# Holding batch 2's loads behind an exponential, and regrouping batch 1's last query turns and scores

## The chip, the core and the metric

The kernel runs on one core of one Trainium2 chip. A core has five engines with a queue each, taken in order: TensorE (PE, matmuls and transposes; PEld is its weight load), VectorE (DVE), ScalarE (ACT), GpSimd (POOL) and SyncE (SP). Here SP and POOL mainly issue DMAs, which 16 DMA engines carry out. The metric is the device time of one launch in microseconds (us): a median of runs, and beside it one profiled execution from which all rows of the trace come.

## The reference

Inputs are `q`, `k`, `v` of 4 batches, 8 heads, 768 tokens, 64 channels, and two weights. Each batch goes through a sparse attention: a token sees the tokens less than 16 away and 24 block summaries (the maximum of 32 keys, the mean of 32 values). A two-layer network with a sigmoid GELU follows.

```python
k_sum = k.reshape(B, H, nb, block, D).max(axis=3)
v_sum = v.reshape(B, H, nb, block, D).mean(axis=3)
mask_l = np.abs(pos[:, None] - pos[None, :]) < window
...
a = np.exp(scores_all)          # local scores (masked) and block scores, less their maximum
a = a / (np.sum(a, axis=-1, keepdims=True) + 1e-09)
out = np.matmul(a, v_all)
...
h = x @ w_in                    # x: tokens x 512, w_in 512 x 2048
g = h * (1.0 / (1.0 + np.exp(-1.702 * h)))
return (g @ w_out)              # w_out 2048 x 512
```

## The kernel before

The four batches are worked one after another, and the attention of a batch is spread among the matmuls of the network for the batch before it. PE has no holes that way. The order of every engine is the order of the program: each wrapped engine (`pe`, `dve`, `act`, `pool`, `sp`) keeps it, and the program writes it out with slots.

Heads are taken in four pairs p = 0 to 3, tokens in two halves of 384. For one batch and one pair:

- `load_batch(b)` issues the loads of a batch on POOL: four for the keys (`load_turned` into two tiles `kb`), twelve for the values (`load_v` into `vw`, one for each of six steps of 128 tokens and each half step), four for the queries (`load_turned` into two tiles `qb`). Before batch 3's loads a one-element copy on POOL into `gate2` reads what a DMA writes, so that POOL waits for it and its loads start no sooner.
- `tq(p, s, eng)` turns the queries of a pair of batch 1 on PE (six transposes into PSUM `ps_t`) and copies them to `qT` on DVE. For batches 2 and 3 `xk` and `xq` turn keys and queries by transposing DMAs on SP, from `kb` into `kx` and from `qb` into `qT`.
- `scores(b, half, p)` makes 12 matmuls into PSUM `ps_s` (two buffers in `psb`, shared by other work) and the exponential on ACT into a tile `a_sb[half, p]`. `mask(half, p)` multiplies that tile in place on DVE. `values(b, half, g)` multiplies two pairs with `vw` on PE and divides on DVE.
- `value_rows(s)` completes `vw` once it is loaded: `halo_dmas` on SP copies edge rows (`vw<-vw`), `vsum` sums blocks of 32 values on PE into `ps_vs` (48 matmuls, six steps of 128 tokens with 8 each), `block_sums` adds them on DVE, and `sum_dmas` spreads them with SP (`vw<-vs`).

The change lies in the output layer of the second half of batch 0, `ff_out(1, ms, part)`: twelve slots of four matmuls into `po`, three row tiles of four parts. After the fourth part of a row tile ACT copies it to `osb` and SP stores it. After each slot `beside(1, i)` does what the table `plan1` names for that slot: `t2` is `tq(2)`, `s02` is `scores` of half 0 and pair 2, `m02` its mask, `v00` the values of half 0 and group 0, `x..` turns of results. After slot 2 the program calls `load_batch(2)`, and after slots 9 and 11 `xk` for the two key tiles of batch 2.

Then the loop over batches begins with b = 1: `ff_open` and `ff_one` are its first layer (`ph`), `value_rows(0)` comes at its second step, `xq` for both query tiles at its third, and `rest_k` (maxima and edges of the keys) at its third to sixth. At its end come batch 2's first scores.

Of the kernel before, what the change touches and what calls it, by code (L numbers as in the profile page):

```python
# [35 lines left out]
def kernel(  # L36
# [30 lines left out]
    pool = _Ordered(tc, nc.gpsimd)  # L67
# [55 lines left out]
    def load_turned(x, b, t2, name, gs_=(0, 1)):  # L123

        for g in gs_:
            t2[g] = castp2.tile([128, 2, NJ, 2, D], BF16, name=name, tag=name)
            for hh in range(2):
                h0 = hh * NP + 2 * g
                pool.dma_start(out=t2[g][:, :, :, hh].rearrange("p i a d -> p (i a) d"),
                               in_=x[b, h0:h0 + 2].rearrange("h (a p) d -> p (h a) d", p=128))  # L130

    def load_v(b):
        w5 = vw[b % 2].rearrange("p (j e) h c -> p j e h c", e=2)
        src = v[b].rearrange("h (j e p) d -> e j p h d", e=2, p=64)
        for j in range(NJ):
            for e in range(2):
                pool.dma_start(out=w5[e * 64:e * 64 + 64, j, e, :, 0:D], in_=src[e, j])
# [106 lines left out]
            eng.memset(v6[g * 32:g * 32 + nb, :, g, D:D + 1], float(block))  # L244

    def load_batch(b):
        if b == 3:
            pool.tensor_copy(out=gate2, in_=qTs[0][:, 0, 0:1])
        load_turned(k, b, kb2, "kb")
        if b == 3:  # L250
            pool.tensor_copy(out=gate2, in_=qTs[0][:, NP - 1, 0:1])
        if b == 1:
            load_turned(q, b, qb2, "qb", (0,))
        load_v(b)
        if b < 3:
            load_turned(q, b, qb2, "qb", (1,) if b == 1 else (0, 1))
# [310 lines left out]
    def xk(g, s):  # L567
        k4 = kxs[s].rearrange("p i (j e) c -> p (i j) e c", e=2)
        src = kb2[g].rearrange("p i a h d -> p (i a h d)")
        for e in range(2):  # L570
            sp.dma_start(out=k4[:, 2 * g * NJ:2 * (g + 1) * NJ, e, e * 64:e * 64 + 64],
                         in_=src[e * 64:e * 64 + 64], transpose=True)
# [13 lines left out]
    a_sb, x_sb, x2 = {}, {}, {}  # L586
# [282 lines left out]
    def ff_out(u, ms, part):  # L869
        if part == 0:  # L870
            po_now[ms] = pmm.tile([128, d_model], F32, name="po", tag="mm")
        po = po_now[ms]
        for nt in range(4 * part, 4 * part + 4):
            pe.matmul(out=po, lhsT=gT[u % 2][:, nt, ms * 128:(ms + 1) * 128],
                      rhs=w_out_sb[:, nt, :], start=(nt == 0), stop=(nt == NT - 1))
        if part == 3:
            osb = outp.tile([128, d_model], F32, name="osb", tag="osb")
            act.activation(out=osb, in_=po, func=ACT.Copy)
            r0 = u * HALF + ms * 128
            sp.dma_start(out=out[r0:r0 + 128, :], in_=osb)  # L880

    gate = consts.tile([128, 2], F32, name="gate")
    gate2 = consts.tile([128, 1], BF16, name="gate2")
# [130 lines left out]
    for e in range(2):  # L1014
        r = slice(64 * e, 64 * e + 64)
        dve.tensor_copy(out=w50[r, JH - e:NJ, e, :, 0:D],
                        in_=v0n[r, :, JH - e:NJ, 0:D].rearrange("p h j d -> p j h d"))
# [3 lines left out]
    for p in range(NP):  # L1021
# [3 lines left out]
    dve.memset(vw[1][:, :, :, D:VC], 1.0)  # L1025
    clear_values(dve, 1)
    load_batch(1)


    plan0 = {1: ["q0", "q1", "q2"], 2: ["s0", "s1", "q3", "m0", "m1"], 4: ["s2", "s3", "m2", "m3"], 6: ["v0", "v1"], 8: ["x0"], 9: ["x1"]}  # L1030

    plan1 = {-1: ["s00", "s01"], 1: ["t2", "m00", "m01"], 2: ["t3", "s02"], 3: ["s03", "m02"], 4: ["m03", "s10"],
             5: ["s11", "m10"], 6: ["v00", "m11", "s12", "s13"], 7: ["v01", "g"], 8: ["m12", "m13"],
             9: ["x00", "x01", "v10"], 10: ["v11"], 11: ["x10"]}

# [20 lines left out]
    def beside(b, slot):  # L1056
        for what in (plan1 if b == 1 else plan).get(slot, ()):
            half, i = int(what[1:2] or 0), int(what[-1:] if len(what) > 1 else 0)
            if what[0] == "t":
                tq(i, 1, dve)  # L1060
            elif what[0] == "m":
                mask(half, i)
            elif what[0] == "g":
                gelu_soon()
            elif what[0] == "R":
                value_rows(1)
            elif what[0] == "s":
                scores(b, half, i)
            elif what[0] == "v":
                values(b, half, i)  # L1070
            elif what[0] == "d":
                dx(half, i)
            else:
                tx(half, i)
# [38 lines left out]
    for i, (ms, part) in enumerate((ms, part) for ms in range(JH) for part in range(4)):  # L1113
        ff_out(1, ms, part)
        beside(1, i)
        if i == 2:
            load_batch(2)
        if i in (9, 11):
            xk(i // 2 - 4, 0)
# [3 lines left out]
    for b in range(1, B - 1):  # L1123
# [32 lines left out]
        i = 0  # L1156
        for t, what in seq:
            product(b, t, what)
            if i == 0:
                g_sums(NT // 2 - 1, dve, (2, 3))  # L1160
            if nxt:
                beside(b + 1, i)
            i += 1
            if nxt and b + 2 < B:
                if i == 1:
                    load_batch(b + 2)
                if i in (16, 18):
                    xk(i // 2 - 8, b % 2)
# [4 lines left out]
    b, n = B - 1, NT // 2  # L1173
# [82 lines left out]
```

## Time and profile before

| what | value |
|---|---|
| median of 3 runs | 205.96 us (205.91 to 206.78) |
| profiled execution, its own time | 205.39 us |
| span of the profile | 203.4 us |
| PE / DVE / ACT / POOL busy | 97% / 69% / 62% / 44% |
| mean granted PE clock | 0.998 |
| output stage with the change (slots 0 to 11) | about 58.2 to 74.5 us of the span |

The span runs from the first to the last instruction of the program; the execution's own time holds 2.0 us more around it. Rows of a timeline give the start and the length in us, the engine, the operation, the tiles (out<-in) and how many were merged, and in brackets the idle time of the engine ahead of them and what ended it. Nearly all instructions carry line 28, the helper that records them, so they are told apart by their tiles. SPq is SP's queue of DMA issues: the length there is that of the issue, not of the transfer.

### The profile page before, as it was taken

The page shows a single profiled execution, that of the slowest core. Times are in us where ns is not written, and L with a number is a line of the kernel's source. Part 1 is how long each engine was busy: PE and PEld are TensorE (multiplying, and loading weights), DVE is VectorE, ACT ScalarE, POOL GpSimd, SP SyncE. Part 2 cuts the span into 40 slices and gives each one's busy share as a digit, 9 for nine tenths or more (in the row PEclk, how much of TensorE's full clock was granted, in tenths as well). Part 3 has the DMA queues.
Part 4 walks back from the last instruction along what each step waited for, and adds up shares of the span by engine and source line. Part 5 has one row for each costly group of instructions (what it writes and reads, how often), then busy time and mean ns, then how long its engine had stood idle before and what let it go on. Part 6 is the DMA issues. An engine that isn't in the chain of part 4 may idle for free.

```text
span 203.4 us, 5851 instructions
## 1 busy us (share of the span) xinstructions
PE 196.7 (97%) x2358; PEld 136.6 (67%) x2358; DVE 141.2 (69%) x391; ACT 125.4 (62%) x240; POOL 89.9 (44%) x141
## 2 busy tenths in 40 slices
PE   6889999999999999999999999999999999999993
PEld 5548655556754566655888876666888865578882
DVE  6586894694856884898767789896769567758221
ACT  4584976638786717777871446778670559984220
POOL 7964489447899584000986034000000009980000
PEclk9999999999999999999999999999999999999999
DMA  5999999999999999999999979999022930000223
GB/s 171 169 165 204 207 207 215 189 156 243 116 122 170 176 170 178 127 165 155 114 181 156 173 140 139 110 247 179 0 104 62 185 119 3 0 0 0 106 105 103
DMA packets 95994, 28.13 MB, mean 138 GB/s; under 512 B 83664, under 2 KB 93152, under 8 KB 95968
## 3 DMA queue, kind: packets, MB, share of 16 engines
q0 software_dynamic: 69648, 13.24, 84.8%
q1 hardware_dynamic: 26176, 14.39, 34.8%
q8 instruction: 18, 0.29, 0.6%
q10 hardware_dynamic: 144, 0.13, 0.2%
q14 instruction: 8, 0.07, 0.1%
HBM read 27.26 MB, written 6.29 MB: 165 GB/s over the span
## 4 chain that ended last, share of the span: by engine, by line
PE 91%; DMA 3%; DVE 3%; issue 1%; ACT 0%; POOLq 0%; DVEq 0%
PE ph L28 32%; PE poA L28 16%; PE po L28 11%; PE poB L28 7%; PE phA L28 4%; PE ps_av L28 4%; PE poC L28 4%; PE ps_s L28 3%; DMA qe<-in_q_dram 3%; DVE ks L28 2%; PE ps_t L28 1%; PE ps_x L28 1%; PE phC L28 1%; PE phB L28 1%; PE phE L28 1%; DVE qT L28 1%
## 5 line engine op out<-in xcount | busy, mean ns | idle before, releaser
L28 PE MATMUL ph<-xT,w_in_sb 128*128 128x384 f16 x400 | 67.8, 326 | 0.1
L28 PEld LDWEIGHTS <-w_in_sb 128*128 128x128 f16 x442 | 42.7, 98 | 27.2 <-issue 0.2
L28 ACT ACTIVATE gT<-ph 128x384 f16<-128x384 f32 x100 | 47.9, 491 | 18.4 <-PE ph L28 17.6
L28 PEld LDWEIGHTS <-gT 128*128 128x128 f16 x312 | 28.8, 98 | 11.3 <-issue 0.2
L28 ACT ACTIVATE a_sb<-ps_s 128x768 bf16<-128x768 f32 (+1 forms) x32 | 25.0, 826 | 12.0 <-PE ps_s L28 12.0
L28 PEld LDWEIGHTS <-gs 128*128 128x128 f16 x288 | 27.7, 98 | 3.4
L28 POOL DMA_DIRECT2D vw<-in_v_dram x36 | 24.6, 699 | 11.9 <-DMA kb<-in_k_dram 5.4
L28 POOL TENSOR_TENSOR gs<-gT 128x384 f16<-128x384 f16 x8 | 7.3, 911 | 43.3 <-ACT gT L28 43.2
L28 PE MATMUL po<-w_out_sb,gT 128*128 128x512 f16 x96 | 23.6, 380 | 0.0
L28 PE MATMUL poA<-ws,gs 128*128 128x256 f16 x144 | 18.7, 273 | 0.0
L28 DVE TENSOR_TENSOR a_sb<-a_sb,mk 128x768 bf16<-128x768 bf16 x28 | 14.9, 554 | 5.5 <-ACT a_sb L28 5.0
L28 DVE TENSOR_TENSOR x<-ps_av,rc 128x384 f16<-128x384 f32 x32 | 17.8, 557 | 1.1
L28 DVE TENSOR_TENSOR gs<-gT 128x384 f16<-128x384 f16 (+1 forms) x34 | 13.3, 390 | 7.2 <-ACT gT L28 6.9
L28 POOL DMA_DIRECT2D qb<-in_q_dram x16 | 15.1, 961 | 2.5 <-DMA w_in_sb<-in_moe_w_in_dram 1.2
L28 PEld LDWEIGHTS <-kx 64*128 64x128 bf16 (+1 forms) x378 | 9.9, 95 | 6.8 <-issue 3.6
L28 POOL DMA_DIRECT2D kb<-in_k_dram x14 | 13.6, 986 | 0.3 <-issue 0.3
L28 DVE TENSOR_REDUCE ks<-kx 128x24 bf16<-128x768 bf16 x12 | 11.4, 948 | 3.4 <-ACT kx L28 3.2
L28 ACT ACT_TABLE_LOAD x10 | 12.8, 1283 | 1.0 <-PEq L1240 0.8
L28 ACT ACTIVATE osb<-poA 128x256 f32<-128x256 f32 x9 | 3.5, 384 | 16.1 <-PE poA L28 16.1
L28 ACT ACTIVATE s<-poA 128x256 f32<-128x256 f32 x11 | 4.2, 385 | 11.2 <-PE poA L28 11.2
L28 PEld LDWEIGHTS <-a_sb 128*64 128x64 bf16 (+2 forms) x400 | 7.9, 108 | 2.8 <-issue 1.3
L28 PE MATMUL poA<-ws,gT 128*128 128x256 f16 x72 | 9.3, 273 | 0.0
(117 smaller groups left out, 288.2 us busy)
## 6 DMA issues: line engine op xcount, KB each, us to landing
out_dram<-osb SPq DMA_DIRECT2D x22, 256.0 KB, 3.9
kb<-in_k_dram POOLq DMA_DIRECT2D x14, 192.0 KB, 6.6
qb<-in_q_dram POOLq DMA_DIRECT2D x12, 192.0 KB, 10.5
vw<-in_v_dram POOLq DMA_DIRECT2D x36, 64.0 KB, 5.5
w_out_sb<-in_moe_w_out_dram POOLq DMA_DIRECT2D x4, 512.0 KB, 12.8
w_in_sb<-in_moe_w_in_dram POOLq DMA_DIRECT2D x3, 512.0 KB, 12.4
vw<-vs SPq DMA_DIRECT2D x6, 198.0 KB, 6.6
gT<-in_k_dram SPq DMA_DIRECT2D x2, 384.0 KB, 3.4
```

The costliest lines, as they stand in the source:

```text
L28: r = f(*a, **kw)
```

## The change

Three edits. In `load_batch`, batch 2's loads get a gate of their own: a one-element POOL copy that reads the exponentials of half 0, pair 2. `load_batch(2)` is called a slot later, after slot 3 instead of slot 2, since those exponentials now come in slot 3. In `plan1` the query turns of pairs 2 and 3 stand together in slot 2 (before: slots 1 and 2), the scores of pairs 2 and 3 together in slot 3 (before: slots 2 and 3), and the masks of both in slot 4 (before: slots 3 and 4), beside the first scores of the other half.

```diff
     def load_batch(b):
+        if b == 2:
+            pool.tensor_copy(out=gate2, in_=a_sb[0, 2][:, 0, 0, 0:1])
         if b == 3:
             pool.tensor_copy(out=gate2, in_=qTs[0][:, 0, 0:1])
         load_turned(k, b, kb2, "kb")
...
-    plan1 = {-1: ["s00", "s01"], 1: ["t2", "m00", "m01"], 2: ["t3", "s02"], 3: ["s03", "m02"], 4: ["m03", "s10"],
+    plan1 = {-1: ["s00", "s01"], 1: ["m00", "m01"], 2: ["t2", "t3"], 3: ["s02", "s03"], 4: ["m02", "m03", "s10"],
              5: ["s11", "m10"], 6: ["v00", "m11", "s12", "s13"], 7: ["v01", "g"], 8: ["m12", "m13"],
              9: ["x00", "x01", "v10"], 10: ["v11"], 11: ["x10"]}
...
         ff_out(1, ms, part)
         beside(1, i)
-        if i == 2:
+        if i == 3:
             load_batch(2)
         if i in (9, 11):
             xk(i // 2 - 4, 0)
```

## The prediction

> **What bounds the kernel now.** I read the page first, then the chain of waits through batch 1's output stage, then POOL, ACT and SP in order of time, then the DMA answers for single issues.
>
> ```profile
> span 203.4 us, 5851 instructions
> PE 196.7 (97%) x2358; PEld 136.6 (67%) x2358; DVE 141.2 (69%) x391; ACT 125.4 (62%) x240; POOL 89.9 (44%) x141
> PEclk9999999999999999999999999999999999999999
> DMA  5999999999999999999999979999022930000223
> ```
>
> TensorE sets the time: it is busy for 97% of the span, at full clock. So an edit can gain only by taking work off PE, and loses when PE has to wait. The DMA engines are busy in nearly every slice of the first 60%, which is where the change works. The chain of waits there (start, length, what):
>
> ```profile
> 58.22 1.83 PE po L28 x8
> 60.06 0.34 PE ps_t L28 x6
> 60.39 0.86 PE po L28 x4
> ...
> 61.59 0.28 PE ps_s L28 x12
> 61.87 0.97 PE po L28 x4
> 62.84 0.28 PE ps_s L28 x12
> ...
> 70.85 0.67 PE ps_x L28 x12
> ...
> 80.33 0.53 PE ps_vs L28 x48
> 80.86 15.71 PE ph L28 x96
> 96.56 0.46 PE ps_s L28 x24
> ```
>
> It is PE from end to end. Two places in it take data from batch 2's loads: `ps_vs` at 80.33 sums the freshly loaded values (vsum), and `ps_s` at 96.56 needs the turned queries. PE takes its work in order, so at either place a late load stops everything behind it. POOL, which issues the loads, in order of time:
>
> ```profile
> 58.49 0.45 POOL L28 COPY kx<-ks 128x288 bf16<-128x288 bf16 x1
> 58.86 4.04 POOL L28 DMA_DIRECT2D kb<-in_k_dram  x4
> ...
> 72.92 1.37 POOL L28 DMA_DIRECT2D vw<-in_v_dram  x2 [0.92 <-DMA vw<-in_v_dram]
> 74.25 4.08 POOL L28 DMA_DIRECT2D qb<-in_q_dram  x4
> 95.86 0.19 POOL L28 COPY gate<-qT 128x1 bf16<-128x1 bf16 x1 [17.53 <-DMA qT<-qb]
> 96.38 4.04 POOL L28 DMA_DIRECT2D kb<-in_k_dram  x4 [0.32 <-issue]
> ...
> 106.45 3.40 POOL L28 DMA_DIRECT2D vw<-in_v_dram  x5 [0.48 <-DMA vw<-in_v_dram]
> ```
>
> Batch 2's loads start at 58.86, as soon as POOL has built batch 1's keys, and the last of twelve value loads is issued at about 73.6 (72.92 and half of the 1.37 for two). The DMA answers for the last value load alone, of batch 2 and then of batch 3 (KB, us from issue to landing):
>
> ```profile
> vw<-in_v_dram POOLq DMA_DIRECT2D x1, 64.0 KB, 6.4
> ...
> vw<-in_v_dram POOLq DMA_DIRECT2D x1, 64.0 KB, 3.0
> ```
>
> So batch 2's values are complete at 73.6 + 6.4 = 80.0, and the first matmul of the sums starts at 80.33. The loop takes the tokens in six steps and only the last step, 8 of 48 matmuls, reads the last load: it starts at 80.33 + 0.53 x 40/48 = 80.77. The loads have **0.8 us** to spare at PE, while the change holds them for several.
>
> **The change part by part.** *The turns and scores.* The two query turns keep their 12 transposes, and the scores keep their 24 matmuls. Two groups of 0.28 become one of 24, which costs 0.46 as in the row at 96.56: 0.10 less. An output group of four after scores costs 0.97 and after other output 0.86, and one such step goes: 0.11 less. Turns next to each other gain nothing (0.67 for 12, 0.34 for 6). That is **-0.2 us** of PE. Bounds: -0.3, if the turns' 0.86 steps shrink as well, and +0.2, because the scores of the next half need the PSUM bank that the third exponentials free, and these come later:
>
> ```profile
> 61.91 0.81 ACT L28 ACTIVATE a_sb<-ps_s 128x768 bf16<-128x768 f32 x1 [1.23 <-PE ps_s L28]
> 62.93 0.60 ACT L28 ACTIVATE osb<-po 128x512 f32<-128x512 f32 x1 [0.20 <-PE po L28]
> ```
>
> *When the hold ends.* On PE the third scores now stand behind four output groups and both turns: 58.22 + 1.83 + 0.86 = 60.91, + 0.67 = 61.58, + 0.86 = 62.44. The fourth output group closes the first row tile, so ACT copies `osb` first (62.93 stood 0.09 behind the end of its group at 62.84; now 62.53, done some 0.5 later because ACT overlaps), then come the third exponentials, 63.05 to 63.86. The scores of the next half reach PE at 62.44 + 0.46 + 0.97 = 63.87, when that bank comes free: a stall of about 0.1 is possible, and it is inside the bounds. POOL's added copy takes 0.19 and the next issue follows 0.52 after its start, as at 95.86 and 96.38. The first key load is issued at 63.86 + 0.52 = **64.4 instead of 58.86, 5.5 us later**. Behind the waiting copy POOL has only the twenty loads of this batch, so nothing else is held; the third pair's mask, which overwrites what the copy reads, must also wait for the copy, 0.2 to 0.5 us, and its reader, the values of the second group, comes three slots later, each of 0.97 at least: no cost. The move of the loads one slot down in POOL's order passes no other POOL instruction.
>
> *What the hold costs.* 5.5 us on a transfer that had 0.8 to spare. Some comes back, because the hold isn't empty for the DMA engines. SP's issues, and the sizes (KB each, us to landing) of a key load, the sums' copies and the first store:
>
> ```profile
> 59.47 1.24 SPq L28 DMA_DIRECT2D vw<-vs  x2
> 63.55 6.23 SPq L28 DMA_DIRECT2D out_dram<-osb  x2
> 69.94 3.52 SPq L28 DMA_TRANSPOSE kx<-kb  x2
> 75.12 0.34 SPq L28 DMA_DIRECT2D out_dram<-osb  x1
> 75.63 3.76 SPq L28 DMA_TRANSPOSE kx<-kb  x2
> ...
> 86.24 9.32 SPq L28 DMA_TRANSPOSE qT<-qb  x2
> ...
> kb<-in_k_dram POOLq DMA_DIRECT2D x14, 192.0 KB, 6.6
> ...
> vw<-vs SPq DMA_DIRECT2D x2, 198.0 KB, 5.1
> ...
> out_dram<-osb SPq DMA_DIRECT2D x1, 256.0 KB, 5.8
> ```
>
> Busy time of each engine, granted clock, then DMA share (over 1 where packets overlap) and GB/s, in three stretches:
>
> ```profile
> 58.86:60.60 1.74, 1.74 (x14) 0.97 (x13) 0.74 (x3) 1.73 (x4) 1.74 (x3) 1.00 0.10 17
> ...
> 60.60:80.00 19.40, 19.40 (x269) 11.09 (x267) 12.76 (x32) 10.79 (x19) 14.53 (x19) 1.00 2.04 174
> 98.00:112.10 14.10, 14.10 (x233) 11.80 (x232) 10.34 (x27) 7.75 (x14) 10.84 (x16) 1.00 1.93 157
> ```
>
> Until 60.6 the engines are nearly idle (17 GB/s); from there to 80.0 they move 174 GB/s. In the new order the two copies of the sums (2 x 198 KB) and the first store (256 KB, issued near 63.2) fall into the hold. These 652 KB at 174 GB/s are 3.8 us which the loads no longer share. They end 5.5 - 3.8 = 1.7 us later: 81.7. On the other side, the key transposes of 75.63 and the third store now fall more into the loads' last microseconds: two transposes of 96 KB each (half of a 192 KB key load) are 1.1 us at that rate; neither none nor all of it is likely, and I take half, 0.55. Values complete: 82.25. PE's last step starts then instead of at 80.77: **+1.5 us**. The 0.2 gained ahead of the wait vanishes into it.
>
> Bounds. From below: batch 3's loads, with no transposes among them, take from 96.38 to the last issue (106.45 + 4/5 of 3.40 = 109.1) + 3.0 = 112.1, 15.7 us; from 64.4 that is 80.1, no wait, so -0.2. From above: nothing comes back, 80.0 + 5.5 = 85.5, +4.7. The value taken lies nearer to the first, since the bytes that leave are counted, and above it since the transposes remain.
>
> *What is late next.* The halo copies, `block_sums`, the sums' copies and the keys' maxima all follow vsum on PE, DVE and SP, and PE is late by the same amount when their data is wanted. The query loads are last in the queue. The turned queries land just ahead of 95.86, when POOL's copy waiting for them ran, and PE wants them at 96.56: 0.7 to spare, plus the 1.5 that PE comes later. Batch 3's loads wait for these queries and are complete at 112.1; the last `ps_vs` of the kernel, which reads them, starts at 124.6, so that spare hides their shift:
>
> ```profile
> L28 PE MATMUL ps_vs<-vw,E x144: 213/216/227, 57.2 to 124.6; 64*32 64x128 bf16 x144
> ```
>
> **Sum.** The profiled execution, 205.39 (span 203.4 and 2.0 around it), becomes 205.39 + 1.5 = 206.9. The median of the runs is 205.96, 0.57 above it, so I predict **207.5**.
>
> **The rivals.**
>
> *No wait (not slower).* The loads go at batch 3's pace and land at 80.1, ahead of PE, and only the 0.2 remains: 205.8. For it: the two rows of batch 3, and 17 GB/s in the hold's first part. Against it: the four key transposes of 69.94 and 75.63 lie in the middle of batch 2's loads; batch 3's stretch has none. It decides while the last value load lands before 80.8.
>
> *The queries become the later ones.* Their loads are behind all others. If only the sums' bytes come back (396 KB at 174 GB/s, 2.3), the queries shift by 5.5 - 2.3 = 3.2, from 95.86 to 99.1, against 96.56: +2.5, 208.5. For it: `qT<-qb` stood on SP for 9.32 us and landed with 0.7 to spare. Against it: those transposes queue behind SP's earlier copies, which do not wait for queries.
>
> *The whole hold passes through*, +4.7, 210.7. For it: the DMA engines are full from 60.6 on. Against it: the 652 KB that leave.
>
> *A stall that slows the clock.* If a stall of that size lets PE's clock drop, the 24 first-layer matmuls behind it, a group of 3.90 us where they stand ahead of the sums, could run at two thirds of their speed: 1.95 more, 212.6. No wait of PE in this trace is longer than 1.3 us, and its clock row is 9 throughout.
>
> ```profile
> 76.43 3.90 PE ph L28 x24
> ...
> PE ps_h L28 <- DVE warm L28: 1.3, 1, 1.3
> ```
>
> The Trainium skill, "TensorE: Matmul & The Clock Gate", Part 1 on the HAM clock gate, says that an idle window of about 3.4 us halves the clock until a busy window has passed; by that an estimate of the extra is 1.7 us, for a stall of 4.7 and not for one of 1.5. No run here shows it yet.
>
> **How the numbers follow.** Forecast 0.45 (207.5), no wait 0.23 (205.8), queries 0.14 (208.5), whole hold 0.13 (210.7), with the clock 0.05 (212.6). The range takes in no wait and the whole hold: 205.5 to 210.8. The forecast's own range is 206.5 (+0.5) to 208.4 (+2.4). About 0.5% (1.03 us) is what can be told from no change. Slower by more: the two longer stalls and the queries, 0.32, and most of the forecast, 0.37: 0.69. Within: the rest of the forecast, 0.08, and no wait but for 0.04: 0.27. Faster, 0.04, would need gains on PE that no row shows.
>
> **What would show it.** Right: first `kb` issue near 64.4 behind a `gate` copy; a PE wait in the middle of `ps_vs`, ending on a DMA of `vw`, of about 1.5 us; a 24-matmul `ps_s` group near 62.4; the last `vw` landing near 82.2; no wait at the next `ps_s`. Wrong: `ps_vs` without a gap (no wait), a gap ahead of batch 2's first `ps_s` (queries), or a last `vw` landing at 85 (whole hold); and wrong altogether if the gate does not move the first `kb` issue.

## The result and the profile after

The changed kernel takes 213.74 us (median of 6 runs, 212.63 to 214.91), the kernel before beside it 206.37. The ratio is 1.0355, 95% interval 1.0297 to 1.0412: **slower by 3.5%**, 7.4 us, and above the range of the prediction. The profiled execution took 212.89 us. A few executions of the kernels further down ran in a slower state; the ratios leave them out, the medians do not. From the page of the changed kernel:

```profile
span 211.1 us, 5853 instructions
PE 199.7 (95%) x2358; PEld 137.6 (65%) x2358; DVE 141.5 (67%) x391; ACT 125.1 (59%) x240; POOL 90.2 (43%) x142
...
PE   6999999999999993699999999999999999999993
...
PEclk9999999999999998599999999999999999999999
```

Two slices of 40, from 79 to 90 us, carry all that can be seen: PE is idle there, and its granted clock dips. POOL in order of time shows the hold as predicted:

```profile
63.46 0.19 POOL L28 COPY gate<-a_sb 128x1 bf16<-128x1 bf16 x1 [4.26 <-ACT a_sb L28]
63.95 4.06 POOL L28 DMA_DIRECT2D kb<-in_k_dram  x4 [0.31 <-PE ps_s L28]
67.97 4.13 POOL L28 DMA_DIRECT2D vw<-in_v_dram  x6
...
74.68 2.71 POOL L28 DMA_DIRECT2D vw<-in_v_dram  x4 [0.54 <-DMA vw<-in_v_dram]
```

The first key load goes out at 63.95, 5.1 us later than before. This trace runs 0.4 us ahead of the one before (batch 1's first scores `ps_s` start at 57.33 instead of 57.77), so against PE's own work the hold is 5.5 us. The chain of waits of the changed kernel, in order of time:

```profile
60.48 0.67 PE ps_t L28 x12
...
62.01 0.46 PE ps_s L28 x24
62.47 0.97 PE po L28 x4
...
76.69 9.77 DMA vw<-in_v_dram
86.46 0.04 issue
86.50 0.30 PE ps_vs L28 x5
86.80 17.16 PE ph L28 x96
103.97 0.46 PE ps_s L28 x24
```

The last value load, issued at 76.69, takes 9.77 us and lands at 86.46, where about 80.0 was the mark before. PE reaches the value sums at 79.69, and its own order of time shows the wait load by load (start, length, what; in brackets the idle time ahead):

```profile
79.69 0.36 PE L28 MATMUL ps_vs<-vw,E 64*32 64x128 bf16 x24
80.86 0.21 PE L28 MATMUL ps_vs<-vw,E 64*32 64x128 bf16 x1 [0.81 <-DMA vw<-in_v_dram]
...
84.07 0.31 PE L28 MATMUL ps_vs<-vw,E 64*32 64x128 bf16 x7 [1.15 <-DMA vw<-in_v_dram]
...
86.50 0.30 PE L28 MATMUL ps_vs<-vw,E 64*32 64x128 bf16 x7 [1.45 <-DMA vw<-in_v_dram]
```

The 7.4 us then add up from two rows of before and after. The first-layer matmuls behind the sums start at 86.80 instead of 80.86, **+5.9** (waits of 5.2 in all, 1.4 more for the sums themselves, which come in seven groups instead of one, and 0.6 less because PE arrived earlier), and the same 96 of them take 17.16 instead of 15.71 us, **+1.45**. Batch 2's first scores stand at 103.97 instead of 96.56: +7.4, and of the span's 7.7 only 0.3 comes later. The windows of the changed kernel say why the 96 are slower (busy time of PE, PEld, DVE, ACT, POOL, then the granted clock, DMA share, GB/s):

```profile
79.00:86.50 7.50, 2.29 (x46) 0.95 (x45) 2.51 (x8) 0.98 (x2) 3.04 (x3) 0.76 2.07 170
86.50:89.70 3.20, 3.20 (x17) 1.57 (x17) 1.43 (x5) 0.68 (x2) 0.00 (x0) 0.50 2.70 152
89.70:92.00 2.30, 2.30 (x16) 1.38 (x15) 0.44 (x2) 1.64 (x4) 0.00 (x0) 0.99 2.10 148
```

After the wait PE is still granted half its clock until 89.7: half of the 2.9 us from 86.8 on is the 1.45.

### The profile page after: what moved, and what is told of

Its sections match the earlier page's. It is cut to its first block, busy times and chain, and to the rows that moved or that the text cites. A ratio compares the mean times of both kernels' runs of the same rounds, so it can differ in the third digit from the quotient of the medians.

```text
span 211.1 us, 5853 instructions
## 1 busy us (share of the span) xinstructions
PE 199.7 (95%) x2358; PEld 137.6 (65%) x2358; DVE 141.5 (67%) x391; ACT 125.1 (59%) x240; POOL 90.2 (43%) x142
## 4 chain that ended last, share of the span: by engine, by line
PE 71%; DMA 19%; POOL 7%; issue 1%; DVE 0%; ACT 0%; POOLq 0%; DVEq 0%
PE ph L28 24%; PE poA L28 15%; DMA vw<-in_v_dram 8%; PE poB L28 7%; PE po L28 6%; DMA w_out_sb<-in_moe_w_out_dram 6%; DMA w_in_sb<-in_moe_w_in_dram 5%; PE phA L28 4%; PE poC L28 4%; PE ps_s L28 3%; POOL kb L28 2%; PE ps_av L28 2%; POOL v0n L28 2%; PE ps_t L28 1%; PE phC L28 1%
## 5 line engine op out<-in xcount | busy, mean ns | idle before, releaser
L28 PE MATMUL ph<-xT,w_in_sb 128*128 128x384 f16 x400 | 69.2, 331 | 0.1
L28 PEld LDWEIGHTS <-w_in_sb 128*128 128x128 f16 x442 | 43.2, 99 | 28.2 <-issue 1.7
```

The costliest lines, as they stand in the source:

```text
L28: r = f(*a, **kw)
```

## The experiments

The theory after this: the hold alone makes the loss, the stall then lowers the clock, and nothing of the hold comes back because the key transposes, whose times hardly moved, now run among the held loads. The rivals: the regrouping, late queries, DMA traffic that slows the matmuls, slow loads as such. All ratios are to the kernel before on the same chip.

**The regrouping alone** (loads free, call after slot 2 as before, `plan1` of the change):

```diff
-    plan1 = {-1: ["s00", "s01"], 1: ["t2", "m00", "m01"], 2: ["t3", "s02"], 3: ["s03", "m02"], 4: ["m03", "s10"],
+    plan1 = {-1: ["s00", "s01"], 1: ["m00", "m01"], 2: ["t2", "t3"], 3: ["s02", "s03"], 4: ["m02", "m03", "s10"],
```

> The kernel before with only the regrouped turns and scores; batch 2's loads start freely at about 58.9 us as before. Theory (the hold alone costs the time): within 0.3 us of the kernel before, -0.2 by the matmul groups, no wait at the value sums. Rival (the regrouping costs some of it, through later exponentials): 1 us or more above the kernel before.

Measured: ratio 0.9970 (0.9936 to 1.0004), 205.54 against 205.83 us. The chain of waits of this kernel runs through the sums without a hole, and the 96 matmuls are at full speed again:

```profile
79.47 0.53 PE ps_vs L28 x48
80.00 15.71 PE ph L28 x96
```

So the regrouping is not to blame. It was repeated with more rounds:

> The regrouping alone once more, to narrow its interval: 0.1 to 0.3% faster than the kernel before (two saved steps on PE, 0.2 us), still within what can be told from no change; rival: no difference at all, ratio 0.999 to 1.001.

Measured: 0.9988 (0.9955 to 1.0022). Both intervals hold 1; the 0.2 us of the prediction cannot be told from nothing here.

**The hold alone** (old `plan1`, call after slot 2):

```diff
     def load_batch(b):
+        if b == 2:
+            pool.tensor_copy(out=gate2, in_=a_sb[0, 2][:, 0, 0, 0:1])
```

> The old order of turns and scores, with only the POOL copy that waits for the third exponentials; these end near 62.7, so the first key load goes out near 63.0, 4.2 us after the kernel before instead of 5.1. Theory: the last value load lands at 85 to 86, PE waits about 4 to 5 us in the value sums and loses 1 to 1.5 more to its clock: 211.5 to 213.5 in all. Rival (the regrouping shares the blame): 209 or less.

Measured: 212.17 us, ratio 1.0290 (1.0222 to 1.0358). Its chain of waits:

```profile
77.37 8.96 DMA vw<-in_v_dram
86.33 0.04 issue
86.37 0.31 PE ps_vs L28 x5
86.68 18.25 PE ph L28 x96
```

This profiled execution started its first matmuls late (batch 1's first scores stand at 58.93, 1.2 us behind the kernel before), so the 86.33 is about 85 on that scale, as expected. PE waits 3.3 us in the sums, less than the 4 to 5 expected, and the 96 matmuls lose 2.5 to the clock, more than the 1 to 1.5 expected. It is the slowest of the four runs; two of the others show a mean granted clock of 0.992 instead of 0.982, so they lost less to it. The hold alone makes most of the loss, 6.3 of 7.4 us, and this hold is about 1 us shorter: the first key load goes out at 64.44, which is 63.3 on the scale of the kernel before.

**The wait moved out of reach**: the changed kernel with batch 2's value sums three steps later on PE.

```diff
-                if n // 2 == 1:
+                if n // 2 == (4 if b == 1 else 1):
                     value_rows(s)
```

> The changed kernel with batch 2's value sums moved three steps later on PE (after its fifth pair of first-layer tiles instead of the second), which is about 87.5 us, behind the last value load at 86.5. Theory (the wait at the sums and the clock behind it are the whole loss): no wait at the sums, clock at 1.0, and the time within 1 us of the kernel before, since SP now turns the queries ahead of the edge copies. Rival (the queries are late as well): a wait of 2 to 4 us ahead of batch 2's first scores, 208.5 to 210.5.

Measured: 205.98 us, ratio 0.9996 (0.9961 to 1.0031), with the hold unchanged: its first key load at 64.05, its last value load landed at 86.3. Its windows show PE busy and at full clock throughout the stretch, and its sums start only at 87.6:

```profile
80.00:87.00 7.00, 7.00 (x45) 4.20 (x43) 5.56 (x20) 5.29 (x11) 2.74 (x3) 1.00 2.00 168
...
L28 PE MATMUL ps_vs<-vw,E x48: 213/216/227, 87.6 to 88.0; 64*32 64x128 bf16 x48
```

So the wait at that one place and the clock behind it are the whole loss. The queries were not late: on SP they stand ahead of the edge copies in this kernel and cost nothing. In the changed kernel, where they stand behind, its own trace has no wait of PE for queries, so the rival of late queries falls.

**The wait filled with matmuls** (their results are not used; they open a new accumulation in the sums' bank, so batch 2's value sums are not the reference's):

```diff
         for j in range(NJ):
             o = EX - 4 * j
+            if s == 0:
+                for _ in range({3: 4, 4: 12, 5: 11}.get(j, 0)):
+                    pe.matmul(out=ps[0][:, 128:512], lhsT=ident, rhs=mk[:, 0:6, :],
+                              start=True, stop=True, skip_group_check=True)
```

> The changed kernel with 27 extra matmuls of 384 columns (results unused) spread over the last three steps of batch 2's value sums, in time that PE spends waiting. Theory (the stall also lowers the clock): the last value load still lands near 86.5 and the sums end near 86.8, but the 96 first-layer matmuls behind them take 15.7 instead of 17.2 us, granted clock near 1.0; 1.3 to 1.5 us faster than the changed kernel, about 212.3. Rival (the slower matmuls come from something else, such as the DMA traffic): still 17.2 us, no faster.

Measured: 211.59 us, ratio to before 1.0242 (1.0175 to 1.0308). The changed kernel had 1.0355 (1.0297 to 1.0412); the two intervals just overlap, so the time alone does not decide it. The trace does. The chain of waits, and the window behind the sums:

```profile
86.21 0.25 PE ps_vs L28 x7
86.46 15.71 PE ph L28 x96
...
86.20:89.70 3.50, 3.49 (x28) 2.13 (x28) 1.43 (x5) 1.96 (x4) 0.00 (x0) 1.00 2.84 156
```

The value loads land as late as ever, the DMA engines are as busy (2.84 against 2.70), and the 96 matmuls are back at 15.71 us. The slow matmuls are a matter of PE's idleness, not of DMA traffic.

**The key transposes moved away** from the value loads, and the keys' maxima two steps later:

```diff
-        if i in (9, 11):
-            xk(i // 2 - 4, 0)
...
                 if n // 2 == 1:
                     value_rows(s)
+                    if b == 1:
+                        xk(0, 0)
+                        xk(1, 0)
...
-                if n // 2 in (2, 3, 4, 5):
-                    rest_k(n // 2 - 2, s)
+                k0 = 4 if b == 1 else 2
+                if n // 2 - k0 in (0, 1, 2, 3):
+                    rest_k(n // 2 - k0, s)
```

> The changed kernel with the four key transposes of batch 2 moved on SP from the output stage (issued at 70.9 to 76.7 us, among the value loads) to behind the edge and sum copies, and the keys' maxima two steps later. Theory (the key transposes, which share the DMA engines packet by packet with the loads, ate the time that the copies and the store gave back): the last value load lands 15 to 16.5 us after the first key load's issue as batch 3's does, at 79 to 80.5, and the value sums wait 0.5 us or less. Rival (the loads alone take 22 us in this stage, or the stores hold them): it lands at 84 to 86.5 and the wait stays 4 us or more. The keys and queries come late in this kernel, so the whole time, 206 to 212, tells little.

Measured: 207.57 us, ratio 1.0096 (1.0069 to 1.0123). The start of POOL's loads, the landing time of the last value load (KB, us from issue), and the sums on PE:

```profile
63.97 4.06 POOL L28 DMA_DIRECT2D kb<-in_k_dram  x4 [0.30 <-PE ps_s L28]
...
74.59 2.71 POOL L28 DMA_DIRECT2D vw<-in_v_dram  x4 [0.41 <-DMA vw<-in_v_dram]
...
vw<-in_v_dram POOLq DMA_DIRECT2D x1, 64.0 KB, 3.0
...
79.70 0.60 PE L28 MATMUL ps_vs<-vw,E 64*32 64x128 bf16 x48
```

The same held loads, issued within 0.1 us of the same times, are done at 76.6 + 3.0 = 79.6 instead of 86.46, and the sums run in one piece. **The four transposes among the loads cost them 6.8 us**, by one profiled execution of each kernel. With them away the loads take 15.7 us from first issue to last landing, batch 3's pace. The time left over, 2 us, is the keys' lateness: DVE waits for the turned keys and PE for DVE.

```profile
DVE ks L28 <- DMA kx<-kb: 2.0, 1, 2.0
PE poA L28 <- DVE s L28: 1.9, 1, 1.9
```

**Half of them moved** (only the second key tile's two):

```diff
-        if i in (9, 11):
-            xk(i // 2 - 4, 0)
+        if i == 9:
+            xk(0, 0)
...
                 if n // 2 == 1:
                     value_rows(s)
+                    if b == 1:
+                        xk(1, 0)
```

> The changed kernel with only the second key tile's two transposing DMAs moved behind the edge and sum copies; the first tile's two stay among the value loads. Theory (each transposing DMA among the loads holds them by a share of its own; four took 6.8 us, from 79.65 to 86.46): last value load near 82 to 84, a wait of 1.5 to 3.5 us in the sums, too short to lower the clock. Rival (one pair alone does the harm): it lands at 79 to 80.5 or at 86.

Measured (2 runs): 211.78 us, ratio 1.0281 (1.0223 to 1.0339). The last value load takes 6.9 us and lands at 83.8, 19.6 after the first key load's issue at 64.18: one pair costs 3.9 and the other 2.9, so each counts. The sums wait 2.6 us in five pieces, and against the expectation the clock falls all the same; DVE's later keys cost 1.5 us of PE besides.

```profile
PE ps_vs L28 <- DMA vw<-in_v_dram: 2.6, 5, 0.9
PE poA L28 <- DVE s L28: 1.5, 1, 1.5
...
84.10:87.00 2.90, 2.90 (x14) 1.39 (x11) 1.43 (x5) 0.67 (x2) 0.00 (x0) 0.50 3.10 146
```

**A shorter hold**, on the first exponentials:

```diff
-            pool.tensor_copy(out=gate2, in_=a_sb[0, 2][:, 0, 0, 0:1])
+            pool.tensor_copy(out=gate2, in_=a_sb[0, 0][:, 0, 0, 0:1])
```

> The changed kernel with the hold shortened: the POOL copy reads the first exponentials (done near 59.7) instead of the third, so the first key load goes out near 60.2 instead of 63.95, 1.4 us after a free start. Theory (whatever is held passes through to the last value load, at least in full): last value load near 80.5 to 82, PE waits 0.5 to 1.5 us in the sums, too short to lower the clock: 206 to 207.5. Rival (the copies and the store in the hold give it back): no wait at all, 205.5. Second rival (only the gate's place among POOL's work matters): as slow as the changed kernel.

Measured: 206.37 us, ratio 1.0040 (1.0023 to 1.0058). The copy went later than expected, since pair 0's mask stands ahead of it in the program and overwrites the tile in place, so that the copy waits for DVE, not ACT:

```profile
60.21 0.19 POOL L28 COPY gate<-a_sb 128x1 bf16<-128x1 bf16 x1 [1.65 <-DVE a_sb L28]
60.69 4.05 POOL L28 DMA_DIRECT2D kb<-in_k_dram  x4 [0.30 <-issue]
...
PE ps_s L28 <- DMA qT<-qb: 0.7, 1, 0.7
PE ps_vs L28 <- DMA vw<-in_v_dram: 0.5, 1, 0.5
```

1.9 us of hold (60.69 against 58.77 in the regrouping alone) move the last value load from 79.0 to 80.9: 1.9, all of it (the loads take 20.2 us in both). PE waits 0.5 at the sums and 0.7 for queries, at full clock.

**Values first**, hold kept:

```diff
+        if b == 2:
+            load_v(b)
         load_turned(k, b, kb2, "kb")
...
-        load_v(b)
+        if b != 2:
+            load_v(b)
```

> The changed kernel, hold kept, with batch 2's value loads issued ahead of its key loads. Theory (the value load's place behind the held keys makes PE wait): the last value load lands at 76 to 79, no wait in the value sums, clock at 1.0; key transposes start 6 to 9 us later and the turned keys and queries come close to batch 2's first scores: 205.5 to 208. Rival (any held load costs the same, the wait only moves to the keys or the queries): a wait of 4 us or more ahead of batch 2's first scores, 210 or more.

Measured: 208.35 us, ratio 1.0129 (1.0088 to 1.0170); a little over the range of the theory, 1.7 us short of the rival's. The values land at 74.3 and the sums run unhindered, but the keys' transposes are issued from 79.1 on and SP's queue turns the queries too late: the first scores of batch 2 wait.

```profile
PE ps_s L28 <- DMA qT<-qb: 3.3, 2, 2.9
...
94.00:98.60 4.60, 1.74 (x11) 0.86 (x10) 4.53 (x18) 3.27 (x6) 0.01 (x1) 1.00 1.20 211
```

No version was found that beats the kernel before; with the wait moved out of reach or the regrouping alone the time is level with it.

## Why the prediction was wrong

The direction was right and the size was not: 7.4 us slower, where 1.5 were forecast.

- *What bounds the kernel*: right. PE had no holes, the sums and the first scores were the two places where a late load could stop it, and the sums did.
- *The turns and scores*: the order came as worked out. The group of 24 stands at 62.01 (62.44 predicted; this trace runs about 0.4 earlier from the start), and the effect on the time lies below what the runs can tell, as said.
- *When the hold ends*: right. 63.95 against 64.4, and with the 0.4 us by which this trace runs ahead the hold is the 5.5 us that were forecast.
- ***What the hold costs* is the step that failed.** It subtracted 3.8 us because the sums' copies and the first store would pass during the hold, and added 0.55 for the key transposes. The copies and the store did pass: in the trace their last packets are moved by 64.3, and the first packet of a load at 65.7. Yet the loads took 22.5 us from first issue to last landing (63.95 to 86.46), where they had taken 21.1 before (58.86 to 80.0) and the prediction had 17.9. They ended 6.5 us later than before, not 1.7 + 0.55.

  The term of the key transposes was mis-sized. Each moves as many bytes as a key load, 192 KB and not 96 (four loads fill the two tiles that four transposes empty). And bytes were the wrong measure: four cost the loads 6.8 us by the run that moved them, 1.7 each, where 192 KB at the 174 GB/s used there would be 1.1. What had gone unseen is that only two of the four ran among the loads before, and all four do after. SP issues them behind its stores of finished row tiles, which the hold does not move: the pairs at 69.94 and 75.63 before, at 70.87 and 75.06 after (the first now waits 1.5 us for the held key loads). So the loads' head start over them shrank from 11.1 to 6.9 us. The transposes' packets, 256 bytes each and 768 to a transpose, show what followed. Before, the first pair's ran from 72.6 to 77.0 and the second pair's only from 80.0 on, when the last value load had landed; after, all four ran from 74.0 to 85.3, ahead of its landing.

```profile
70.87 3.00 SPq L28 DMA_TRANSPOSE kx<-kb  x2
74.55 0.35 SPq L28 DMA_DIRECT2D out_dram<-osb  x1
75.06 4.34 SPq L28 DMA_TRANSPOSE kx<-kb  x2
```

  The run with half of them moved prices the second pair among the loads at 2.9 us, where the prediction had 0.55. The loads grew by 1.4 only; if the first pair cost the same before and after, an estimate of what the copies and the store gave back is 1.5 us instead of 3.8. No run moves the copies or the store alone, so that part stays open.

- The lower bound, batch 3's pace of 15.7 us, was the true pace without key transposes; the row stood there with the reason why it didn't apply, and was still given more weight than the upper bound. That stretch was not wholly free of transposes: one of results, `xT<-x`, was issued at 110.51 and began within its last microsecond.
- *What is late next*: right in the changed kernel, whose next scores did not wait. With a short hold and with values first the queries did become late, by 0.7 and 3.3 us.
- *The rivals*: the whole hold together with the lowered clock, given 0.05, comes nearest: 212.6 worked out, 213.74 measured. That it comes so near is partly luck. It let the 5.5 us pass through as they were, while the loads took 1.4 us longer on top; the sums ended 5.9 us later instead of 4.7, and the clock cost 1.45 instead of 1.95. Its two thirds of the speed stood on no row; the trace shows half the clock, and 2.9 us of it fell on the 96 matmuls. The Trainium skill, "TensorE: Matmul & The Clock Gate", Part 1, quoted there, gave an estimate of 1.7. The idle window of about 3.4 us on which that rests did not occur: PE's longest wait was 1.45.

## What to carry to other kernels

Before holding a transfer, look for what shares the DMA engines with it and is not held, and ask which of the two moves against the other; counting bytes at the mean rate hides that. A load that lands 0.8 us ahead of an in-order engine leaves no room for a hold; moving its reader later (the sums, three steps) bought 8 us of room at no cost that the runs could tell. When PE is to stall for a few microseconds, price the slow clock that may follow as well.

## What the hardware showed unasked

**DMA transposes among plain loads.** Four transposes of 192 KB made 15.7 us of loads into 22.5. The Trainium skill, "DMA: Bandwidth & Descriptors", Latency and other measured facts, has an effective 261 GB/s for a DMA transpose with a non-contiguous middle dimension; by that an estimate for 4 x 192 KB is 3.0 us. The 6.8 us that the loads lost are more than that, but they are not the same quantity. No run here times the transposes by themselves, so how the loss splits between their own time and what they do to the loads stays open.

**The clock falls without a long idle stretch.** In the changed kernel no single wait is over 1.5 us, and with half of the transposes moved none is over 0.9, yet the clock went to half; there PE was busy for 2.29 of 7.50 us and 1.52 of 4.10. The row of the second, with half of the transposes moved:

```profile
80.00:84.10 4.10, 1.52 (x49) 0.71 (x50) 1.79 (x7) 0.49 (x1) 3.05 (x3) 0.96 2.26 189
```

One wait of 2.9 us, with values first, left the clock at 1.00, though PE was busy for 1.74 of 4.60 us there, much the same share. So neither the longest wait nor the share over the whole stall decides.

The traces' record of the granted clock narrows it down. It is half from 82.90 to 89.73 in the changed kernel, from 84.99 to 91.81 with the hold alone, and from 83.81 to 87.22 with half of the transposes moved: 6.83, 6.83 and 3.41 us. The stretch at full clock ahead of each lasted 78.51 us, 23 times 3.41. So the clock changed on a grid of 3.41 us in these runs. In the 3.41 us just ahead of the drop PE was busy for 1.21, 1.21 and 0.92 us. On the same grid the wait with values first is cut in two at 97.04, and PE was busy for 2.11 and 1.86 us of the two steps. By these rows a step with little work is enough, and how the stall lies on the grid seems to matter. The Trainium skill, "TensorE: Matmul & The Clock Gate", Part 1, speaks of an idle window of about 3.4 us; the length agrees with the 3.41 here, but PE was not idle through it. Where the limit lies between 1.21 and 1.86 us was not tried, nor whether the sums' small matmuls (64 rows by 32 columns) count for less.
